# Attention and a routed expert layer on one core: blocks turned two at a time, other places for the expert buffers, longer value rows and a shorter cut of GpSimd's work

## The chip, the cores and the metric

The kernel runs on one core of one Trainium2 chip. The metric is the device time of one execution in microseconds; the kernel before takes 766.43 us (median of three runs, 765.69 to 766.94). Engines are named as the profile names them: PE is TensorE (PEld its weight loads), DVE VectorE, ACT ScalarE, POOL GpSimd, SP the queue that issues most DMAs.

## The reference, cut to what matters

```python
# attention: B=8, H=8, S=576, D=64; a query block of 64 rows sees the key blocks up to its own
scores = scale * np.matmul(q, k.transpose(0, 1, 3, 2))
mask = block_i >= block_j                      # blocks of 64
scores = np.where(mask, scores, -1000000000.0)
attn = np.exp(scores - np.max(scores, axis=-1, keepdims=True))
attn = attn / (np.sum(attn, axis=-1, keepdims=True) + 1e-09)
x = (attn @ v).transpose(0, 2, 1, 3).reshape(B * S, H * D)     # 4608 rows of 512
# one expert of 8 for each row
logits = x @ w_gate + modality_bias[modality_id]
e_idx = np.argmax(logits, axis=1)              # gate_w: softmax of the logits at e_idx
for e in range(E):
    mask = e_idx == e
    h = np.maximum(x[mask] @ w1[e], 0.0)       # 512 -> 1024
    out[mask] = gate_w[mask, None] * (h @ w2[e])   # 1024 -> 512
```

## The kernel before

**Attention** goes through 32 pairs of heads, one pair in a slot; 33 slots are walked, and `ORDER` lists by hand in which order every slot hands work to the engines. Each engine works its own list strictly in that order. The two heads of a pair lie in the two halves of the 128 partitions.

In its slot a pair is taken through these steps (letters as in `ORDER`):

- `S`, `M`, `E` (scores, row maxima, exponentials). The nine query blocks, called subs 0 to 8, have 64 to 576 keys. `PIECES` cuts the scores into ten column stretches, `COL` says in which of the six PSUM banks each stands, and `UNITS` groups them for DVE's maxima and ACT's exponentials. Sub 8 has 576 columns and needs two banks; `CUT` is where it is cut. PE multiplies 64x64 tiles, and the subs in `FLIP` use the other two quarters of its array, so that two subs run side by side. The exponentials go to `pm`, one column stretch for each sub (`OFF`).
- `G`, `g`: nine small gate products from `vt`, copied by ACT into the columns 64 to 71 of each 73-column block of the value tile `v`. The last column of a block is 1, which makes the row sums.
- `T`, `C` (turn and copy). PE transposes `pm` in 128-column blocks, a matmul with the identity as the moving operand, into PSUM; ACT or DVE (`ON_DVE`) copies it to `pt`. `GROUPS` lists the blocks of each of seven groups. An even sub has an odd number of 64-column halves, so its last block has only 64 columns: these five are the half-height blocks, in groups 5 and 6. Group 6 (sub 0 alone) is turned first, into the bank that group 5 uses last.
- `Va`, `Vb`, `Za`, `Zb` belong to the pair of the slot before: PE multiplies `pt` with `v` (50 products), DVE divides by the row sums into `xr`.
- `q...` are the steps of routing (logits, expert, place in the expert's list), mostly small DVE operations, done for a batch while the next batch's slots run. POOL scatters the row numbers by indirect DMA.

**The last seven slots of attention** also prepare the first expert: `EARLY_STEPS` stages its weights through two 128x1024 buffers (`staging`); `prep` lets POOL cast each to float32r (high part) and subtract it from the original (low part), into `extra`. DVE works beside that.

**The expert layer** takes segments of 256 rows: 10 of expert a and c with weights in `extra` (name "a"), 8 and a half of expert b with weights in `w0hb`, `w0lb`, `w1b`. A segment is 8 transposes (`turn_rows`), 96 products of 256 moving columns (`up_products`; stationary: a weight block, moving: `xth` or `xtl`) and 48 products of 512 moving columns (`down`; stationary: a block of `hidden`, moving: the second weights). In `extra` every buffer begins at a multiple of 4,096 bytes from its start. In the program as built, `extra` starts at byte 28,288 of a partition (a multiple of 64), `w0hb` at 156,192 and `w1b` at 188,960 (each 32 more than a multiple of 64).

Of the kernel before, what the change touches and what calls it, by code (L numbers as in the profile page):

```python
# [11 lines left out]
F32 = mybir.dt.float32  # L12
# [38 lines left out]
PIECES = (((7, 0, 512),), ((6, 0, 448), (0, 0, 64)), ((5, 0, 384), (3, 0, 256)), ((8, 0, 256), (4, 0, 320), (8, 256, 576), (2, 0, 192), (1, 0, 128)))  # L51
# [6 lines left out]
GBANK = (0, 1, 2, 3, 4, 5, 5)  # L58
POS = {x: 512 * g + 128 * i for g, group in enumerate(GROUPS) for i, x in enumerate(group)}
# [44 lines left out]
def attention_moe(ctx, tc, qk, vr, vt, gmw, mid, mb, w1, w2, cf, ci, ld, out):  # L104
# [30 lines left out]
    extra = steady.tile([128, 22 * 1024], F32R, name="extra")  # L135
# [14 lines left out]
    pms = [att.tile([128, OFF[-1] + S], F32, name=f"pm{i}") for i in range(2)]  # L150
# [3 lines left out]
    for v in vs:  # L154
        dve.memset(v[:, :, D + NE], 1.0)
    for t in pts:
        dve.memset(t[64:128, 512 * HALF :], 0.0)
# [26 lines left out]
    def place(s, a, b):  # L184
        i, o = COL[s] if a == 0 else (COL[s][0] + 1, -CUT)
        return banks[i][:, o + a : o + b]
# [332 lines left out]
class Experts:  # L519
    def __init__(self, ctx, tc, cst, scratch, btmp, edges, xrows, idlist, idf, w1, w2, out, sel, run, base8, pick, dot, banks, ys, placing, staging, extra, xrb):  # L520
# [223 lines left out]
    def run_all(self, steps):  # L744
# [101 lines left out]
def _prepare(q, k, v, moe_modality_id, moe_w_gate, moe_modality_bias, moe_w1, moe_w2):  # L846
# [28 lines left out]
```

## Time and profile before

| | us |
|---|---|
| median of three runs | 766.43 |
| profiled execution, its own time | 774.59 |
| its span, first to last instruction | 772.9 |
| attention, to the first expert transposes | about 317 |
| one slot, most of them | 9.40 |
| one expert segment, a / b | about 23.3 / 23.6 |

The profiled execution is 8.2 us slower than the median, so durations are summed against 774.59 and the difference is then taken from 766.43. "Busy" of PE counts a matmul's modelled end, so PE looks busy in every stretch where it is fed; the starts of successive instructions tell more. A wait in brackets is the idle time of that engine just before the row, with what ended it.

### The profile page before, as it was taken

The page shows a single profiled execution, that of the slowest core. Times are in us where ns is not written, and L with a number is a line of the kernel's source. Part 1 is how long each engine was busy: PE and PEld are TensorE (multiplying, and loading weights), DVE is VectorE, ACT ScalarE, POOL GpSimd, SP SyncE. Part 2 cuts the span into 40 slices and gives each one's busy share as a digit, 9 for nine tenths or more (in the row PEclk, how much of TensorE's full clock was granted, in tenths as well). Part 3 has the DMA queues.
Part 4 walks back from the last instruction along what each step waited for, and adds up shares of the span by engine and source line. Part 5 has one row for each costly group of instructions (what it writes and reads, how often), then busy time and mean ns, then how long its engine had stood idle before and what let it go on. Part 6 is the DMA issues. An engine that isn't in the chain of part 4 may idle for free. (4 is left out here: it accounts for less than half of the span.)

```text
span 772.9 us, 20835 instructions
## 1 busy us (share of the span) xinstructions
PE 752.9 (97%) x8696; PEld 669.2 (87%) x8696; DVE 371.9 (48%) x1095; ACT 323.0 (42%) x685; POOL 165.4 (21%) x146
## 2 busy tenths in 40 slices
PE   7999999999999999998999999999999999999995
PEld 5888888888888877988999999999999888999894
DVE  4888888888899999643111221111221222221120
ACT  4777776777776766412212222212221222221220
POOL 0000202020202466217223223223112211112101
PEclk9999999999999999998999999999999999999998
DMA  7478565656565969331221221122212212211000
GB/s 206 129 222 229 147 179 149 175 151 177 154 182 132 248 192 268 86 79 36 66 83 69 83 69 70 40 83 70 74 51 83 83 55 69 69 42 46 28 14 19
DMA packets 82625, 85.12 MB, mean 110 GB/s; under 512 B 53002, under 2 KB 64970, under 8 KB 82528
## 3 DMA queue, kind: packets, MB, share of 16 engines
q1 hardware_dynamic: 75040, 64.24, 30.5%
q0 software_dynamic: 7488, 19.52, 7.9%
q8 instruction: 69, 1.13, 0.6%
q14 instruction: 28, 0.23, 0.1%
HBM read 62.09 MB, written 22.25 MB: 109 GB/s over the span
## 5 line engine op out<-in xcount | busy, mean ns | idle before, releaser
L681 DVE SCALAR_TENSOR_TENSOR extra<-bank,extra 128x512 fp32r<-128x512 f32 x72 | 49.8, 691 | 316.7 <-ACT extra L680 316.7
L216 ACT ACTIVATE pm<-bank,nm 128x320 f32<-128x320 f32 (+3 forms) x320 | 137.0, 508 | 70.0 <-DVE nm L208 68.2
L674 PE MATMUL bank<-extra 128*128 128x256 f32 x960 | 121.8, 288 | 2.7 <-issue 2.2
L674 PEld LDWEIGHTS bank<-extra 128*128 128x128 f32 x960 | 119.5, 196 | 5.0 <-issue 3.8
L208 DVE TENSOR_REDUCE nm<-bank 128x1 f32<-128x256 f32 (+7 forms) x288 | 110.8, 444 | 12.0 <-PE bank L200 11.6
L680 ACT ACTIVATE extra<-bank 128x512 fp32r<-128x512 f32 x72 | 43.1, 598 | 165.5 <-PE bank L674 156.6
L226 PE MATMUL bank<-cf,pm 128*128 128x128 f32 (+1 forms) x800 | 95.1, 277 | 2.7 <-ACT pm L216 2.2
L367 POOL DMA_INDIRECT idlist<-idt,pi x40 | 39.4, 986 | 251.6 <-DVE pi L366 162.0
L674 PE MATMUL bank<-extra,w0hb 128*128 128x256 f32 x512 | 92.5, 282 | 0.0
L226 PEld LDWEIGHTS bank<-cf,pm 128*128 128x128 f32 (+1 forms) x800 | 86.6, 136 | 5.8 <-ACT pm L216 3.8
L200 PE MATMUL bank<-raw,q 64*64 64x256 f32 (+7 forms) x1280 | 87.0, 408 | 0.0
L200 PEld LDWEIGHTS bank<-raw,q 64*64 64x64 f32 x1280 | 54.6, 133 | 29.3 <-issue 19.0
L674 PEld LDWEIGHTS bank<-extra,w0hb 128*128 128x128 f32 x512 | 79.2, 188 | 0.7
L231 ACT COPY pt<-bank 128x512 f32<-128x512 f32 (+1 forms) x128 | 64.5, 504 | 27.5 <-PE bank L226 24.8
L250 PE MATMUL o<-v,pt 128*64 128x73 f32 x2048 | 75.1, 228 | 0.0
L674 PE MATMUL bank<-extra,w0lb 128*128 128x256 f32 x256 | 71.9, 281 | 0.0
L231 DVE COPY pt<-bank 128x512 f32<-128x512 f32 (+1 forms) x96 | 64.8, 684 | 14.2 <-PE bank L226 12.8
L250 PEld LDWEIGHTS o<-v,pt 128*64 128x64 f32 x2048 | 70.3, 136 | 0.1
L720 PE MATMUL o<-extra 128*128 128x512 f32 x240 | 57.1, 393 | 0.0
L720 PE MATMUL bank<-extra 128*128 128x512 f32 x240 | 56.0, 389 | 0.0
L720 PEld LDWEIGHTS bank<-extra 128*128 128x128 f32 x240 | 45.0, 188 | 9.4
L720 PE MATMUL o<-w1b,extra 128*128 128x512 f32 x216 | 52.8, 400 | 0.0
(146 smaller groups left out, 819.1 us busy)
## 6 DMA issues: line engine op xcount, KB each, us to landing
raw<-qk SPq DMA_DIRECT2D x31, 576.0 KB
v<-vr SPq DMA_DIRECT2D x32, 320.0 KB
vt<-vt SPq DMA_DIRECT2D x32, 288.0 KB
xrows<-xr SPq DMA_DIRECT2D x16, 576.0 KB
staging<-w SPq DMA_DIRECT2D x24, 256.0 KB
staging<-w SPq DMA_DIRECT2D x12, 512.0 KB
idlist<-btmp SPq DMA_DIRECT2D x8, 304.0 KB
idlist<-idt,pi POOLq DMA_INDIRECT x40
```

Of the source, the lines that this page charges most:

```text
L200: pe.matmul(place(s, a, b)[64 * t : 64 * t + 64], d.q[hs, D * s : D * s + D], d.k[hs, a:b], start=True, stop=True)
L208: dve.tensor_reduce(low, place(s, a, b), AX.X, ALU.max, negate=True)
L216: act.activation(d.pm[:, OFF[s] + a : OFF[s] + b], place(s, a, b), AF.Exp, bias=d.nm[:, s : s + 1], scale=1.0)
L226: pe.transpose(banks[GBANK[g]][0:m, 128 * i : 128 * i + 128], d.pm[:, o : o + m], idf)
L231: dve.tensor_copy(dst, src) if g in ON_DVE else act.copy(dst, src)
L250: pe.matmul(o[64 * h : 64 * h + 64], d.pt[:, a : a + 64], d.v[:, 5 * h + j, :], start=j == 0, stop=j == s // 2)
L367: last = pool.indirect_dma_start(idlist[:], bass.IndirectOffsetOnAxis(ap=g.pi[c], axis=0), g.idt[:, c, :], None, bounds_check=NROW - 1, oo ...
L674: nc.tensor.matmul(hp[:, a, :], w[:, kc, ms], x[:, kc, :], start=i == 0, stop=i == len(mm) - 1)
L680: self.nc.scalar.activation(hh, hp, AF.Relu)
L681: self.nc.vector.scalar_tensor_tensor(hl, hp, 0.0, hh, ALU.max, ALU.subtract)
L720: nc.tensor.matmul(y, s.hs[m][x][:, ts], self.part(w, 1, m // 2)[:, m % 2, :], start=n == 0, stop=n == len(mm) - 1)
```

## The change

Five edits, all in one file:

1. Turning. `pm` gets a new layout: the last 64 columns of sub 6 stand just ahead of sub 0, those of sub 4 just ahead of the last 64 columns of sub 8 (`TAIL`). One 128-column transpose then turns two half-height blocks at once, the second into the upper 64 partitions of the bank. The 25 transposes of a pair become 23. Group 6 has no transposes of its own any more; its copy (`C6`, now 256 columns) reads partitions 64 to 127 of bank 5 and writes partitions 0 to 63 of `pt`, at the end of the turn, and group 5's copy loses a quarter of its columns.
2. Scores. Sub 8 is cut at 512 instead of 256: 512 columns fill bank 4, the last 64 go to bank 5 with subs 3 and 1.
3. Buffers. `extra` is laid out anew, with the first weights of expert a (`w["a", 0]`) last and 32 bytes further; two 32-byte pads stand around `w1b`. As built, `w0hb` is at byte 156,128 (still 32 more than a multiple of 64) and `w1b` at 188,928 (a multiple of 64).
4. Values. The host lays out `v` with its gate columns and ones, so one pair's load is one run of 2,920 bytes a partition instead of ten runs of 256. Three memsets go.
5. `prep`. POOL casts and subtracts in four pieces of 256 columns, a cast and a subtraction in turn.

```diff
+SHIFT = 8
-COL = {7: (0, 0), 6: (1, 0), 0: (1, 448), 5: (2, 0), 4: (3, 0), 2: (3, 320), 3: (4, 0), 8: (4, 256), 1: (5, 320)}
-CUT = 256
+COL = {7: (0, 0), 6: (1, 0), 0: (1, 448), 5: (2, 0), 4: (3, 0), 2: (3, 320), 8: (4, 0), 3: (5, 0), 1: (5, 256)}
+CUT = 512
+LONG = (5, 384)
-OFF = [32 * s * (s + 1) for s in range(NSUB)]
+OFF = {7: 0, 5: 512, 3: 896, 1: 1152, 6: 1280, 0: 1728, 4: 1792, 8: 2176, 2: 2688}
+TAIL = 2112
 GROUPS = (
...
-    ((3, 0), (3, 1), (2, 0), (1, 0)), ((6, 3), (4, 2), (2, 1), (8, 4)), ((0, 0),),
+    ((3, 0), (3, 1), (2, 0), (1, 0)), ((6, 3), (4, 2), (2, 1)), ((0, 0), (8, 4)),
 )
 ORDER = (
...
-    ("T6", 0), ("C6", 0), ("T0", 0), ("C0", 0), ...
+    ("T0", 0), ("C0", 0), ... ("T5", 0), ("C5", 0), ("C6", 0), ...
@@ attention_moe
-    extra = steady.tile([128, 22 * 1024], F32R, name="extra")
+    extra = steady.tile([128, 22 * 1024 + SHIFT], F32R, name="extra")
-    for v in vs:
-        dve.memset(v[:, :, D + NE], 1.0)
@@ load_v
-        nc.sync.dma_start(d.v[:, :, 0:D], vr[p].rearrange("p (a d) -> p a d", d=D))
+        nc.sync.dma_start(d.v.rearrange("p a f -> p (a f)"), vr[p][:, 0 : 10 * VW])
@@ transposes
-        m = height(g)
         for i, (s, j) in enumerate(GROUPS[g]):
             o = OFF[s] + 128 * j
-            pe.transpose(banks[GBANK[g]][0:m, 128 * i : 128 * i + 128], d.pm[:, o : o + m], idf)
+            m = 64 if s == 2 and j == 1 else 128
+            pe.transpose(banks[g][0:m, 128 * i : 128 * i + 128], d.pm[:, o : o + m], idf)
@@ copies
+        if g < HALF:
+            dst, src = pt[:, 512 * g : 512 * g + n], banks[g][:, 0:n]
+        elif g == HALF:
+            dst, src = pt[0:64, LOW : LOW + n], banks[HALF][0:64, 0:n]
+        else:
+            dst, src = pt[0:64, LOW + 384 : LOW + 384 + n], banks[HALF][64:128, 0:n]
@@ Experts
-        self.w["a", 0] = [cut(4096 * x, 4, 4096) for x in range(2)]
-        self.w["a", 1] = [[cut(1024 * (8 + 4 * x + c), 2) for c in range(4)] for x in range(2)]
-        self.xth, self.xtl = cut(1024 * 16, 4), cut(1024 * 17, 4)
-        self.hidden = [[cut(1024 * (18 + i) + 512 * x, 2, 512) for x in range(2)] for i in range(4)]
+        self.w["a", 1] = [[cut(1024 * (4 * x + c), 2) for c in range(4)] for x in range(2)]
+        self.xth, self.xtl = cut(1024 * 8, 4), cut(1024 * 9, 4)
+        self.hidden = [[cut(1024 * (10 + i) + 512 * x, 2, 512) for x in range(2)] for i in range(4)]
+        self.w["a", 0] = [cut(1024 * 14 + SHIFT + 4096 * x, 4, 4096) for x in range(2)]
@@ early, "prep"
-            self.nc.gpsimd.tensor_copy(self.target(k, name, c)[0], st)
-            self.lower(True)
+            flat = [t.rearrange("p a f -> p (a f)") if len(t.shape) > 2 else t for t in (st, *self.target(k, name, c))]
+            for i in range(4):
+                s, h, l = (t[:, 256 * i : 256 * i + 256] for t in flat)
+                self.nc.gpsimd.tensor_copy(h, s)
+                self.nc.gpsimd.tensor_tensor(l, s, h, ALU.subtract)
+            self.staged.pop(0)
@@ run_all
+        wk.tile([128, SHIFT], F32R, name="pad0")
         w2 = [wk.tile([128, 2, DM], F32R, name=f"w1b{i}") for i in range(8)]
+        wk.tile([128, SHIFT], F32R, name="pad1")
```

How the instructions stand now. On PE, the turn of one pair and the first scores of the next slot, before (`bank_90` to `bank_95` are the six banks in order, `pm` the exponentials, `cf` holds the identity; 64x128 is a half-height block; a wait stands in brackets):

```order
L250 MATMUL b_97<-v_104,pt_109 64x73 x17
L226 MATMUL bank_95<-cf,pm_108 64x128 [waits Activation_49]
L226 MATMUL bank_90<-cf,pm_108 128x128 x4
L226 MATMUL bank_91<-cf,pm_108 128x128 x4
L226 MATMUL bank_92<-cf,pm_108 128x128 x4
L226 MATMUL bank_93<-cf,pm_108 128x128 x4
L226 MATMUL bank_94<-cf,pm_108 128x128 x4
L226 MATMUL bank_95<-cf,pm_108 64x128 [waits Activation_49]
L226 MATMUL bank_95<-cf,pm_108 64x128 x3
L200 MATMUL bank_90<-raw_98,q_100 64x512 [waits DMAHW3_49,Activation_49]
```

and the same place in the change (its lines are numbered otherwise: L255 was L250, L225 was L226, L201 was L200):

```order
L255 MATMUL b_97<-v_104,pt_109 64x73 x17
L225 MATMUL bank_90<-cf,pm_108 128x128 x4
L225 MATMUL bank_91<-cf,pm_108 128x128 x4
L225 MATMUL bank_92<-cf,pm_108 128x128 x4
L225 MATMUL bank_93<-cf,pm_108 128x128 [waits Activation_49]
L225 MATMUL bank_93<-cf,pm_108 128x128 x3
L225 MATMUL bank_94<-cf,pm_108 128x128 x3
L225 MATMUL bank_94<-cf,pm_108 128x128 [waits Activation_49]
L225 MATMUL bank_95<-cf,pm_108 128x128 x2
L225 MATMUL bank_95<-cf,pm_108 64x128
L201 MATMUL bank_90<-raw_98,q_100 64x512 [waits DMAHW3_49,Activation_49]
```

Two transposes are gone, and the first wait for ACT's exponentials stands twelve transposes later. On ACT, from the last exponentials of a pair to the first of the next, before (`q` is the scaled query, `nm` the negated maxima):

```order
L216 ACTIVATE pm_107<-bank_95,nm 128x128 [waits Activation_49]
L182 ACTIVATE q_101<-raw_99 128x576 [waits DMAHW6_49,Activation_49]
L231 COPY pt_109<-bank_95 64x128 [waits PE_49]
L231 COPY pt_109<-bank_90 128x512 [waits PE_49,Activation_49]
L231 COPY pt_109<-bank_92 128x512 [waits PE_49,Activation_49]
L231 COPY pt_109<-bank_94 128x512 [waits PE_49,Activation_49]
L216 ACTIVATE pm_108<-bank_90,nm 128x512 [waits DVE_49]
```

and in the change:

```order
L218 ACTIVATE pm_107<-bank_95,nm 128x128 [waits Activation_49]
L183 ACTIVATE q_101<-raw_99 128x576 [waits DMAHW6_49,Activation_49]
L236 COPY pt_109<-bank_90 128x512 [waits PE_49,Activation_49]
L236 COPY pt_109<-bank_92 128x512 [waits PE_49,Activation_49]
L236 COPY pt_109<-bank_94 128x512 [waits PE_49]
L236 COPY pt_109<-bank_95 64x256 [waits DVE_49]
L218 ACTIVATE pm_108<-bank_90,nm 128x512 [waits DVE_49]
```

The copy of group 6 moved from the head of the copies to their end, is twice as wide, and waits for DVE, whose copy of group 5 reads the other half of the same bank.

## Rows read from the trace of the kernel before

**Rows 1.** Windows, a slot: length, busy PE, PEld, DVE, ACT, POOL; clock, DMA share, GB/s.
```profile
17.10:26.50 9.40, 9.40 (x188) 8.19 (x187) 7.83 (x22) 6.85 (x17) 0.00 (x0) 1.00 0.44 130
```

**Rows 2.** Timeline of PE in that slot: start us, us, instruction, idle before.
```profile
17.08 2.69 PE L200 MATMUL bank<-raw,q 64*64 64x512 f32 x40
...
23.63 2.92 PE L226 MATMUL bank<-cf,pm 128*64 128x128 f32 x25
26.48 1.08 PE L200 MATMUL bank<-raw,q 64*64 64x512 f32 x8
```

**Rows 3.** Timeline of PE's weight loads, part of a turn: full blocks, half blocks.
```profile
166.90 1.23 PEld L226 LDWEIGHTS bank<-cf,pm 128*128 128x128 f32 x11
...
168.75 0.33 PEld L226 LDWEIGHTS bank<-cf,pm 128*64 128x64 f32 x3
```

**Rows 4.** Groups by form: ACT's copies of the turn, busy us and mean ns.
```profile
L231 ACT COPY pt<-bank 128x512 f32<-128x512 f32 x96 | 56.3, 586 | 25.5 <-PE bank L226 23.6 <-issue 0.9 <-ACT pt L231 0.6
...
L231 ACT COPY pt<-bank 64x128 f32<-64x128 f32 x32 | 8.2, 257 | 2.0 <-PE bank L226 1.2
```

**Rows 5.** Timeline of PEld and DVE where a slot begins.
```profile
159.87 0.21 PEld L200 LDWEIGHTS bank<-raw,q 64*64 64x64 f32 x8 [0.20 <-issue]
160.05 0.68 DVE L231 COPY pt<-bank 64x512 f32<-64x512 f32 x1 [0.25 <-PE bank L226]
```

**Rows 6.** Timeline of PE and DVE where the slot of the expert choice begins.
```profile
236.10 0.40 PEld L200 LDWEIGHTS bank<-raw,q 64*64 64x64 f32 x8 [0.20 <-issue]
236.58 1.27 DVE L231 COPY pt<-bank 128x512 f32<-128x512 f32 x2
```

**Rows 7.** Waits: who for whom, us in all, times, longest.
```profile
PEld bank L226 <- ACT pm L216: 3.8, 8, 2.3
```

**Rows 8.** Timeline of the first slot, PE and ACT.
```profile
9.63 0.72 PE L238 MATMUL b<-gm,vt 128*64 128x16 f32 x18 [0.58 <-DMA vt<-vt]
...
10.94 1.56 ACT L216 ACTIVATE pm<-bank,nm 128x256 f32<-128x256 f32 x4
12.39 0.69 ACT L182 ACTIVATE q<-raw 128x576 f32<-128x576 f32 x1
12.56 4.58 PE L226 MATMUL bank<-cf,pm 128*64 128x128 f32 x25 [2.21 <-ACT pm L216]
```

**Rows 9.** Windows: the turn of the first slot.
```profile
12.50:17.10 4.60, 4.54 (x29) 4.35 (x29) 1.38 (x2) 2.24 (x6) 0.00 (x0) 0.63 0.74 217
```

**Rows 10.** Timeline around 283 us: POOL, DVE, PE.
```profile
282.79 2.36 POOL L618 TENSOR_TENSOR extra<-staging,extra 128x1024 fp32r<-128x1024 f32 x1
282.99 2.17 DVE L366 TENSOR_TENSOR pi<-pp,cf 128x1 int32<-128x1 f32 x1
286.18 0.44 PE L291 MATMUL b<-l,cf 128*128 128x72 f32 x2 [1.48 <-DVE l L288]
```

**Rows 11.** Timeline around 303 us: DVE, PE.
```profile
302.96 2.27 DVE L333 TENSOR_SCALAR sm<-sm 128x5 f32<-128x5 f32 x1
307.57 0.20 PE L326 MATMUL b<-oh,ones 128*128 128x40 bf16 x1 [1.39 <-DVE row L563]
```

**Rows 12.** Timeline of PE: a segment of expert a, then parts of two of b.
```profile
505.06 5.73 PE L720 MATMUL o<-extra 128*128 128x512 f32 x24
516.06 11.68 PE L674 MATMUL bank<-extra 128*128 128x256 f32 x96
527.57 1.03 PE L656 MATMUL bank<-cf,xr 128*128 128x128 f32 x8
539.36 0.40 PE L674 MATMUL bank<-extra,w0hb 128*128 128x256 f32 x2
550.88 1.04 PE L656 MATMUL bank<-cf,xr 128*128 128x128 f32 x8
551.67 5.87 PE L720 MATMUL o<-w1b,extra 128*128 128x512 f32 x24
562.99 0.40 PE L674 MATMUL bank<-extra,w0hb 128*128 128x256 f32 x2
```

More of the change, by code (lines that the diff above doesn't have):

```diff
@@ L47 @@
 UNITS = ((7,), (6, 0), (5,), (4, 2), (3, 8, 1))
-COL = {7: (0, 0), 6: (1, 0), 0: (1, 448), 5: (2, 0), 4: (3, 0), 2: (3, 320), 3: (4, 0), 8: (4, 256), 1: (5, 320)}
-CUT = 256
+COL = {7: (0, 0), 6: (1, 0), 0: (1, 448), 5: (2, 0), 4: (3, 0), 2: (3, 320), 8: (4, 0), 3: (5, 0), 1: (5, 256)}
+CUT = 512
+LONG = (5, 384)
 FLIP = (6, 0, 5, 4, 2)
-PIECES = (((7, 0, 512),), ((6, 0, 448), (0, 0, 64)), ((5, 0, 384), (3, 0, 256)), ((8, 0, 256), (4, 0, 320), (8, 256, 576), (2, 0, 192), (1, 0, 128)))
-OFF = [32 * s * (s + 1) for s in range(NSUB)]
+PIECES = (((7, 0, 512),), ((6, 0, 448), (0, 0, 64)), ((5, 0, 384), (8, 0, 512)), ((4, 0, 320), (3, 0, 256), (2, 0, 192), (8, 512, 576), (1, 0, 128)))
+OFF = {7: 0, 5: 512, 3: 896, 1: 1152, 6: 1280, 0: 1728, 4: 1792, 8: 2176, 2: 2688}
+TAIL = 2112
 GROUPS = (
     ((7, 0), (7, 1), (7, 2), (7, 3)), ((6, 0), (6, 1), (6, 2), (5, 0)), ((5, 1), (5, 2), (4, 0), (4, 1)), ((8, 0), (8, 1), (8, 2), (8, 3)),
-    ((3, 0), (3, 1), (2, 0), (1, 0)), ((6, 3), (4, 2), (2, 1), (8, 4)), ((0, 0),),
+    ((3, 0), (3, 1), (2, 0), (1, 0)), ((6, 3), (4, 2), (2, 1)), ((0, 0), (8, 4)),
 )
 HALF = 5
-GBANK = (0, 1, 2, 3, 4, 5, 5)
-POS = {x: 512 * g + 128 * i for g, group in enumerate(GROUPS) for i, x in enumerate(group)}
+LOW = 512 * HALF
+POS = {x: 512 * g + 128 * i - 128 * (g > HALF) for g, group in enumerate(GROUPS) for i, x in enumerate(group)}
 ON_DVE = (1, 3, 5)
@@ L149, in attention_moe @@
     vs = [att.tile([128, 10, VW], F32, name=f"v{i}") for i in range(3)]
-    pms = [att.tile([128, OFF[-1] + S], F32, name=f"pm{i}") for i in range(2)]
+    pms = [att.tile([128, D * NSUB * (NSUB + 1) // 2], F32, name=f"pm{i}") for i in range(2)]
     pts = [att.tile([128, 25 * 128], F32, name=f"pt{i}") for i in range(2)]
@@ L153, in attention_moe @@
     dve.memset(zeros, 0.0)
-    for v in vs:
-        dve.memset(v[:, :, D + NE], 1.0)
     for t in pts:
-        dve.memset(t[64:128, 512 * HALF :], 0.0)
+        dve.memset(t[64:128, LOW:], 0.0)
     scatters, placing = [], []
@@ L184, in place @@
     def place(s, a, b):
-        i, o = COL[s] if a == 0 else (COL[s][0] + 1, -CUT)
-        return banks[i][:, o + a : o + b]
+        i, o = COL[s] if a == 0 else LONG
+        return banks[i][:, o : o + b - a]
     def spans(s):
@@ L215, in exps @@
             for a, b in spans(s):
-                act.activation(d.pm[:, OFF[s] + a : OFF[s] + b], place(s, a, b), AF.Exp, bias=d.nm[:, s : s + 1], scale=1.0)
-    def height(g):
-        return 64 if g >= HALF else 128
+                o = OFF[s] if a == 0 else TAIL
+                act.activation(d.pm[:, o : o + b - a], place(s, a, b), AF.Exp, bias=d.nm[:, s : s + 1], scale=1.0)
     def transposes(p, g):
         d = pairs[p]
-        m = height(g)
         for i, (s, j) in enumerate(GROUPS[g]):
             o = OFF[s] + 128 * j
-            pe.transpose(banks[GBANK[g]][0:m, 128 * i : 128 * i + 128], d.pm[:, o : o + m], idf)
+            m = 64 if s == 2 and j == 1 else 128
+            pe.transpose(banks[g][0:m, 128 * i : 128 * i + 128], d.pm[:, o : o + m], idf)
     def copies(p, g):
-        m, n = height(g), 128 * len(GROUPS[g])
-        dst, src = pairs[p].pt[0:m, 512 * g : 512 * g + n], banks[GBANK[g]][0:m, 0:n]
+        pt = pairs[p].pt
+        n = 128 * len(GROUPS[g])
+        if g < HALF:
[4 more added lines that the diff above has]
+            dst, src = pt[0:64, LOW + 384 : LOW + 384 + n], banks[HALF][64:128, 0:n]
         dve.tensor_copy(dst, src) if g in ON_DVE else act.copy(dst, src)
@@ L850, in _prepare @@
     vp = v.reshape(NPAIR, 2, S, D)
-    vr = np.zeros((NPAIR, 128, 2, 5, D), v.dtype)
-    vr[:, :, :, 0:4] = vp[:, :, 0:512].reshape(NPAIR, 2, 4, 128, D).transpose(0, 3, 1, 2, 4)
-    vr[:, 0:64, :, 4] = vp[:, :, 512:576].transpose(0, 2, 1, 3)
+    vr = np.zeros((NPAIR, 128, 2, 5, VW), v.dtype)
+    vr[..., VW - 1] = 1
+    vr[:, :, :, 0:4, 0:D] = vp[:, :, 0:512].reshape(NPAIR, 2, 4, 128, D).transpose(0, 3, 1, 2, 4)
+    vr[:, 0:64, :, 4, 0:D] = vp[:, :, 512:576].transpose(0, 2, 1, 3)
     gmw = np.zeros((2, D, PPB, 2 * NE), moe_w_gate.dtype)
```

2 lines of the change are left out of this document (1 added, 1 removed), and 2 rows, old and new, of the table ORDER.

## The prediction, made before the result was known

> **What bounds the kernel now.** I read the page's slices first, then the windows of one slot, PE's timeline in it, the waits, and last the timelines of the first slot, of the slots in which POOL prepares weights, and of two expert segments. In the slices the reader is to see PE full from one end to the other, and in an ordinary attention slot the window says it outright: PE 9.40 of 9.40 us, DVE 7.83, ACT 6.85 [rows 1]. The slot runs from one pair's first score product at 17.08 to the next one's at 26.48; the turn starts at 23.63 and fills what is left [rows 2]. So PE's own instructions set the time of attention, and DVE has some 1.6 us of slack a slot. The expert layer is PE alone.
>
> **Turning in twos.** It removes four half-height transposes a pair and makes two others full: 25 become 23. What a half-height one is worth is the point: three half loads in a row take 0.33 us, eleven full ones 1.23 [rows 3]. That is 0.11 us each, both ways; the identity that streams through is 128 columns long in either. Two fewer are 0.22 us a slot, over 32 slots 7.0 us, all on the path. The slot should come to 9.18. The Trainium skill ("TensorE: Matmul & The Clock Gate", section LDWEIGHTS) says that a load costs by its stationary columns, so that a half block would cost half: by it 22.5 block loads stay 22.5 and the sum would lose the 7.0. The rows above speak against it here, since the halves are no closer together than the whole ones.
>
> The scores keep their ten pieces and 2,880 columns a head; the two quarters of the array get 1,472 and 1,408 columns as before, so I price the new cut of sub 8 at nothing on PE. On ACT and DVE it trades 256 + 320 columns for 512 + 64, which their slack hides.
>
> **The copy that moved.** Group 6's copy grows from 128 to 256 columns: between 257 and 586 ns [rows 4], by the line between them 0.37 us, 0.11 more. It now stands last in ACT's turn copies and waits for DVE's copy of group 5. Behind it on ACT are the next pair's exponentials, which wait for maxima anyway; on PE the pieces of bank 5 (subs 3, 8's tail, 1) wait for it, and everything behind them. DVE's copy ends 0.86 us after the slot's start (159.87 to 160.73) [rows 5], and loses a quarter of its columns; so group 6 is copied by about 1.2. PE asks for bank 5 at about 1.6: in its quarter 1,024 of 1,472 columns go ahead, of some 2.4 us, and the weights load a little earlier (an estimate from the scores' row). That leaves 0.35 us of slack. It is gone where routing holds DVE up: in the slot of the expert choice, begun at 236.10, DVE's last copy ends at 237.85 [rows 6], so group 6 ends near 2.0 and PE loses 0.4. I charge 0.6 for this slot and three lesser ones; the ends are nothing and the whole 7.0. A copy from one partition half to the other is not in the trace before; see the slower rival.
>
> **The first wait of the turn.** Before, the first transpose used bank 5 and so waited for the pair's last exponential. Now twelve transposes, 1.3 us, go ahead of the first such wait. The view of waits has 3.8 us in eight such waits, the longest 2.3 [rows 7]; that one is the first slot. The other seven make 1.5; part of each is a pause that PE makes between products and transposes anyway, so I take 0.9 (ends 0 and 1.5).
>
> **The first slot** has no products of an earlier pair to fill PE. The gates end at 10.35 (9.63 + 0.72), the turn starts at 12.56 after 2.21 us idle, ACT's last exponential ends at 12.50 (10.94 + 1.56) and its scaling of the next query at 13.08 [rows 8]. In the change twelve transposes run from 10.4 to 11.7, sub 8's wait until its exponential at about 12.0, the last until 12.5, and the turn ends near 13.1. The next scores then wait for ACT's first copy, 13.08 + 0.59 = 13.7 [rows 4], instead of 17.08. Of these 3.3 us, 0.2 are counted above and 0.4 go because banks 2 and 4 are copied only by 14.3 and 14.9. I take 2.7. The old turn also ran in part at the lower of PE's two clock levels: the granted clock was 0.63 over that stretch, after the idle time before it [rows 9]. With that idle time mostly gone I expect 2.4 GHz; at 1.2 GHz over the new turn and the scores behind it the gain would be 1.0, so the ends are 1.0 and 3.1.
>
> The value loads become fewer, longer runs; nobody waits for them in an ordinary slot, and the DMA engines are at 0.44 [rows 1], so: nothing. ACT's gate copy must now wait for its pair's load, with the last exponentials behind it; the load is issued a slot ahead, so that too is nothing, except in the first slot, within the bounds just given. The three memsets stood under DVE's wait for the first query.
>
> **POOL in four pieces.** At 282.99 a DVE operation on one column took 2.17 us, until POOL's subtraction of 2.36 us was over; PE then waited 1.48 us for DVE [rows 10]. At 302.96 the same happened to a five-column one, 2.27 us, and PE waited 1.39 us [rows 11]. A quarter of the subtraction is 0.6 us, and that much DVE's 1.6 us of slack absorbs. I take both waits as gone, 2.9 us; the ends are nothing (if POOL's pieces follow so closely that DVE gets no turn between them) and 2.9. What eight instructions instead of two cost POOL is not shown; between two preparations it mostly waits for DMAs, so I price it at nothing.
>
> **The expert buffers.** The same 48 down products take 11.00 us in a segment of expert a (505.06 to 516.06) and 11.32 in one of b (551.67 to 562.99) [rows 12]. Instructions and shapes are alike; what differs is where the operands lie: in a, `hidden` and the second weights both start at multiples of 64 bytes, in b the weights start 32 further. The change puts `w1b` at a multiple of 64, so I expect b to become like a: 0.32 us in eight and a half segments, 2.7 us. The 96 up products take 11.51 us in a (516.06 to 527.57) and 11.52 in b (539.36 to 550.88) [rows 12], where the weights already stand 32 bytes off; so moving a's to 32 off is worth nothing. No row shows the new addresses themselves. The only address effect in sight is 0.32 of 11.0, 2.9%: for the ups of 18 segments that is 6.0 us either way, and for a's down products, whose distance modulo 64 stays, 3.2 the wrong way.
>
> The Trainium skill ("TensorE: Matmul & The Clock Gate", section Step-by-step: what each phase is for) gives weight loads and moving operand a read port each and says that one doesn't slow the other. By that the pads would do nothing and the 2.7 us go. The row has a difference between a and b that it does not explain, hence my choice, but the rule stands as a rival.
>
> **Sum.** 7.0 + 0.9 + 2.7 + 2.9 - 0.6 + 2.7 = 15.6 us. The profiled execution's 774.59 would become 759.0; the runs' median is 8.2 lower, and I take the same 15.6 from it: 766.43 - 15.6 = 750.8.
>
> **Rivals.**
> - The pads do nothing (the rule on read ports): 15.6 - 2.7 = 12.9 us, 753.5. For it: up products don't care about 32 bytes. Against it: the 0.32 us. Chance 0.20.
> - The turn's saving does not come, because bank 5 comes free 0.2 us too late in every slot or because half blocks were cheap: 750.8 + 7.0 = 757.8. Against it: 0.35 us of slack, and the spacing of the half loads. Chance 0.08.
> - POOL's pieces still shut DVE out: 750.8 + 2.9 = 753.7, and later still where several DVE operations are hit in a row. For it: DVE runs many small operations there. Chance 0.06.
> - The new places quicken the up products too: 6.0 us at 2.9%, 744.8; if they came down to the transposes' 0.11 us from 0.12, 96 products by 18 segments would give 17 us, 733. Nothing in the rows calls for it, but nobody would see it there either. Chance 0.10.
> - Slower: ACT's copy from the upper partitions to the lower ones costs far more than its size. From 0.72 us on (0.37 + 0.35) PE waits for bank 5 in each of 32 slots, and from 1.21 us on (15.6 / 32 more) the kernel is slower than before; at 1.3 us it would be 32 x 0.58 = 18.6 against 15.6, 769.4. Against it: the widest copy of the turn takes 0.59 us. Chance 0.04.
>
> The forecast keeps 0.52, with a range of its own of 747 to 754. The range of 743 to 758 takes in all but the slower rival and the far end of the quicker one. A measurement of this kernel can tell about 0.2%, 1.5 us, from no change; the slower rival is all that lies beyond it upward, 0.04, some mixture of failures could end near 766, 0.03, and 0.93 is left for faster.
>
> **What would show it.** In the profile after: ordinary slots 9.18 us apart; 23 transposes; the first slot's next scores near 13.7; granted clock at full in the first slot; no DVE operation of 2 us near 283 or 303 us, and no PE wait for routing there; b's 48 down products in 11.0 us; ups still 11.5. Slots that stay at 9.40 with PE waiting at bank 5 would prove the second rival, or the last. Slots of 9.18 with a segment of b still 11.32 would prove the first.

## The result, and the profile after

The kernel after takes 753.29 us (median of six runs, 752.61 to 756.76) where the kernel before takes 767.0 (six runs, 765.69 to 769.10): a ratio of 0.983, 95% interval 0.981 to 0.985. The forecast was 750.8, the range 743 to 758. The profiled execution took 752.61, span 751.0. From the starts on PE, stretch by stretch, in us (slots are counted from 0):

| stretch | before | after | less |
|---|---|---|---|
| to the first score product | 6.36 | 5.42 | 0.9 |
| first slot | 10.72 | 7.71 | 3.0 |
| next 25 slots | 239.22 | 234.46 | 4.8 |
| slots 26 to 30 (POOL prepares weights) | 51.41 | 47.52 | 3.9 |
| last slot, to the first ups | 11.14 | 11.18 | 0.0 |
| first ups to last downs | 434.27 | 424.48 | 9.8 |
| rest | 19.8 | 20.2 | -0.4 |

These 22 us are more than the 13.7 of the medians. The profiled execution before was 8.2 above the median shown with it, and 6.3 us of the expert layer's 9.8 are one stall in it, near 355 us, that the profile after does not have (below). The 0.9 at the start is no part of the change either: the kernel after has 6.25 there in its second profile. Without these two about 15 are left. An ordinary slot after, first the window with the columns of [rows 1], then PE's timeline:

```profile
22.50:31.72 9.22, 9.22 (x186) 7.96 (x185) 8.39 (x28) 7.07 (x17) 0.00 (x0) 1.00 0.44 139
```

```profile
31.69 2.70 PE L201 MATMUL bank<-raw,q 64*64 64x512 f32 x40
...
38.25 2.73 PE L225 MATMUL bank<-cf,pm 128*128 128x128 f32 x23
40.91 1.50 PE L201 MATMUL bank<-raw,q 64*64 64x512 f32 x16
```

The slot is 9.22 (31.69 to 40.91), not 9.40, and the turn 2.73 instead of 2.92 [rows 2]. PE still sets it. The first slot, where [rows 8] has the turn from 12.56 to 17.1, and its window:

```profile
9.72 1.53 PE L225 MATMUL bank<-cf,pm 128*128 128x128 f32 x12
11.62 1.42 PE L225 MATMUL bank<-cf,pm 128*128 128x128 f32 x11 [0.38 <-ACT pm L218]
13.14 1.07 PE L201 MATMUL bank<-raw,q 64*64 64x512 f32 x10
```

```profile
9.72:13.14 3.42, 2.95 (x26) 2.45 (x24) 2.11 (x6) 3.17 (x10) 0.00 (x0) 1.00 1.00 376
```

Twelve transposes go ahead of the exponentials that were the first wait, and the granted clock is 1.00 where [rows 9] has 0.63. The moved copy and the waits around it, from the groups by form and the view of waits:

```profile
L236 ACT COPY pt<-bank 64x256 f32<-64x256 f32 x32 | 11.8, 369 | 15.1 <-DVE pt L236 15.0
```

```profile
ACT pt L236 <- DVE pt L236: 15.0, 31, 1.6
PEld bank L201 <- ACT pt L236: 1.0, 3, 0.5
PEld bank L225 <- ACT pm L218: 0.6, 1, 0.6
```

It takes 0.37 us, and ACT waits for DVE 31 times; PE only three times. [Rows 7]'s 3.8 us are now 0.6. The dearest of the three is in slot 22:

```profile
208.63 3.42 PE L201 MATMUL bank<-raw,q 64*64 64x512 f32 x40
208.91 0.65 DVE L350 RECIPROCAL wt<-sm 128x80 f32<-128x80 f32 x1
209.48 1.08 DVE L236 COPY pt<-bank 128x512 f32<-128x512 f32 x2
210.65 0.37 ACT L236 COPY pt<-bank 64x256 f32<-64x256 f32 x1 [1.65 <-DVE pt L236]
```

A routing step stands ahead of DVE's last two copies, so group 6 is copied at 211.0, and the scores take 3.42 instead of 2.70. Near 283 us, where [rows 10] has a DVE operation of 2.17:

```profile
283.29 0.73 POOL L562 TENSOR_TENSOR extra<-staging,extra 128x256 fp32r<-128x256 f32 x1
283.80 0.23 DVE L371 TENSOR_TENSOR pi<-pp,cf 128x1 int32<-128x1 f32 x1
```

And the expert segments that answer to [rows 12], expert a first, then b:

```profile
496.12 11.52 PE L683 MATMUL bank<-extra 128*128 128x256 f32 x96
507.48 1.03 PE L665 MATMUL bank<-cf,xr 128*128 128x128 f32 x8
508.27 5.73 PE L729 MATMUL o<-extra 128*128 128x512 f32 x24
...
519.28 0.40 PE L683 MATMUL bank<-extra,w0hb 128*128 128x256 f32 x2
...
531.34 5.82 PE L729 MATMUL o<-w1b,extra 128*128 128x512 f32 x24
...
542.57 0.40 PE L683 MATMUL bank<-extra,w0hb 128*128 128x256 f32 x2
...
553.84 1.04 PE L665 MATMUL bank<-cf,xr 128*128 128x128 f32 x8
```

From start to start: a's ups 11.36 (were 11.51), a's downs 11.01 (11.00), b's downs 11.23 (11.32), b's ups 11.27 (11.52; over the eight segments 11.26 to 11.40). So b's downs did **not** come down to 11.0, and the ups, predicted to stay at 11.5, did change. That is the open question.

### The profile page after: what moved, and what is told of

Read it like the earlier page. It is cut to its first block, busy times and chain, and to the rows that moved or that the text cites. A ratio compares the mean times of both kernels' runs of the same rounds, so it can differ in the third digit from the quotient of the medians.

```text
span 751.0 us, 20660 instructions
## 1 busy us (share of the span) xinstructions
PE 736.7 (98%) x8632; PEld 653.9 (87%) x8632; DVE 362.9 (48%) x1092; ACT 328.9 (44%) x685; POOL 172.3 (23%) x194
## 5 line engine op out<-in xcount | busy, mean ns | idle before, releaser
L218 ACT ACTIVATE pm<-bank,nm 128x64 f32<-128x64 f32 (+3 forms) x320 | 135.9, 504 | 49.4 <-DVE nm L209 45.4
L209 DVE TENSOR_REDUCE nm<-bank 128x1 f32<-128x512 f32 (+7 forms) x288 | 119.5, 475 | 15.6 <-PE bank L201 15.3
L683 PE MATMUL bank<-extra 128*128 128x256 f32 x960 | 116.1, 281 | 1.2 <-ACT extra L668 0.9
L683 PEld LDWEIGHTS bank<-extra 128*128 128x128 f32 x960 | 115.0, 188 | 2.4 <-issue 1.1
L225 PE MATMUL bank<-cf,pm 128*128 128x128 f32 (+1 forms) x736 | 87.7, 275 | 0.4 <-ACT pm L218 0.4
L201 PE MATMUL bank<-raw,q 64*64 64x64 f32 (+7 forms) x1280 | 87.7, 409 | 0.1
L225 PEld LDWEIGHTS bank<-cf,pm 128*128 128x128 f32 (+1 forms) x736 | 78.9, 139 | 3.2 <-ACT pm L218 0.6
L201 PEld LDWEIGHTS bank<-raw,q 64*64 64x64 f32 x1280 | 53.0, 133 | 31.7 <-issue 24.2
L236 ACT COPY pt<-bank 128x512 f32<-128x512 f32 (+1 forms) x128 | 67.4, 535 | 28.3 <-DVE pt L236 15.0
L255 PE MATMUL o<-v,pt 128*64 128x73 f32 x2048 | 75.3, 228 | 0.2 <-issue 0.2
L255 PEld LDWEIGHTS o<-v,pt 128*64 128x64 f32 x2048 | 70.4, 136 | 0.5 <-issue 0.3
L236 DVE COPY pt<-bank 128x512 f32<-128x512 f32 (+1 forms) x96 | 60.9, 640 | 7.3 <-PE bank L225 2.9
L732 POOL DMA_INDIRECT out<-scratch,ids_b x17 | 17.1, 1003 | 161.7 <-ACT scratch L731 161.7
L729 PEld LDWEIGHTS bank<-extra 128*128 128x128 f32 x240 | 45.0, 188 | 9.4
```

What stands on the lines that cost most here:

```text
L201: pe.matmul(place(s, a, b)[64 * t : 64 * t + 64], d.q[hs, D * s : D * s + D], d.k[hs, a:b], start=True, stop=True)
L209: dve.tensor_reduce(low, place(s, a, b), AX.X, ALU.max, negate=True)
L218: act.activation(d.pm[:, o : o + b - a], place(s, a, b), AF.Exp, bias=d.nm[:, s : s + 1], scale=1.0)
L225: pe.transpose(banks[g][0:m, 128 * i : 128 * i + 128], d.pm[:, o : o + m], idf)
L236: dve.tensor_copy(dst, src) if g in ON_DVE else act.copy(dst, src)
L255: pe.matmul(o[64 * h : 64 * h + 64], d.pt[:, a : a + 64], d.v[:, 5 * h + j, :], start=j == 0, stop=j == s // 2)
```

## The experiments

Each stood beside runs of the kernel before on its own chip; that kernel alone was 767 us beside the result and on chip 9, and 772 on chips 1, 4 and 8, so ratios are compared, and stretches of traces. "Last slot" is the stretch from the start of slot 31 to the first ups, 11.2 us in the profile after.

**Products alone.** Two kernels that only multiply: blocks of ups (`w` stationary, `x` streamed) and of downs (`h`, in the place of `x`, stationary, `d`, in the place of `w`, streamed), with one pair of starting places after another. `x` and `h` are operand 1, moved by `f` words, `w` and `d` operand 2, moved by `g`.

```diff
+for n, (f, g) in enumerate(SHIFTS):
...
+                    pe.matmul(banks[a % 2][:, 0:256], w[u][:, kc, ms], x[v][:, kc, :], start=i == 0, stop=i == len(mm) - 1)
...
+                    pe.matmul(banks[2 + a], h[m // 2][x][:, m % 2, 128 * a : 128 * a + 128], d[u][:, m, :], start=i == 0, stop=i == len(mm) - 1)
```

> Products alone: nothing of attention, routing or experts is computed, only 22 times 48 up-like products (128x128 weights, 256 moving columns) and 48 down-like ones (512 moving columns), one pair of starting places after another. The weights of the ups (the moving operand of the downs) start 0, 4, 8, 16, 24, 32, 48, 64, 96, 128, 192, 216, 224, 232, 256, 384, 512 and 768 words of 4 bytes past a common place; the last four pairs move the other operand by 8, both by 8, the other by 224, and none. Theory (places modulo 64 bytes): distances of 0, 16, 32, 48 ... words are alike, 8 and 24 are alike and differ from them: downs near 227 ns at the first kind and 234 at the second, ups 120 and 118. Rival 1 (places matter, but modulo something longer): 224 words, the distance that expert b's second weights have to the hidden rows in the kernel after, gives 234 ns for downs although it is a multiple of 64 bytes, and 0 gives 227. Rival 2 (places do not matter, the rule that weight loads and moving operand have a port each): all distances within 1 ns, and what differs in the kernels comes from the other engines, which stand still here.

> Products alone again (48 up-like and 24 down-like ones for each set of places; nothing of attention, routing or experts is computed). Four places are moved apart: the high and the low part of the operand that the ups stream (both also the weights of the downs), and the high and the low part of the other. In words of 4 bytes: (0,0,0,0); both parts of the first operand by 2, 4, 6, 8, 10, 12, 16, 24, 32, 40, 48, 56, 60, 72, 136, 264; then (8,0,0,0), (0,8,0,0), (8,16,0,0), (8,40,0,0), (0,0,0,8), (0,0,8,0), (0,0,0,32), (8,8,0,8), (8,8,8,0), (8,8,0,32), (8,8,0,56), (8,8,256,256), (0,0,24,24), (0,0,216,216). Theory (the distance of the two operands modulo 64 words, that is 256 bytes, sets the spacing): 72, 136 and 264 give what 8 gives, 116.7 ns for ups, 216 what 24 gives, and no place gives downs under 226.7. Rival (absolute places or longer distances count too): they differ by over 1 ns from what 8 gives.

PE's timelines of the first (operand 2 moved by 216, then by 224) and of the second (operand 1 by 40, then by 48):

```profile
195.06 5.80 PE L51 MATMUL bank<-buf 128*128 128x256 f32 x48
200.69 11.38 PE L57 MATMUL bank<-buf 128*128 128x512 f32 x48
211.91 5.92 PE L51 MATMUL bank<-buf 128*128 128x256 f32 x48
217.67 11.36 PE L57 MATMUL bank<-buf 128*128 128x512 f32 x48
```

```profile
122.39 5.86 PE L51 MATMUL bank<-buf 128*128 128x256 f32 x48
128.08 5.75 PE L56 MATMUL bank<-buf 128*128 128x512 f32 x24
133.67 5.62 PE L51 MATMUL bank<-buf 128*128 128x256 f32 x48
139.12 5.66 PE L56 MATMUL bank<-buf 128*128 128x512 f32 x24
```

Start to start over 48, the ups take 117.3 and 120.0 ns, then 118.5 and 113.5: no other engine works. By how far operand 1 lies past operand 2, in words of 4 bytes, modulo 64, the spacing from start to start, where it repeats steadily, is:

| | 0 | 8 | 16 | 24 | 32 | 40 | 48 | 56 | 60 |
|---|---|---|---|---|---|---|---|---|---|
| ups, ns | 120.0 | 116.7 | 117.8 | 120.0 | 118.7 or 120.0 | 117.3 or 118.7 | 113.3 or 117.8 | 118.4 | 117.1 or 118.3 |
| downs, ns | 226.7 | 233.2 | 233.3 | 234.3 | 232.2 or 233.5 | 233.3 | 228.9 | 233.3 | 226.7 or 231.8 |

Moves by 72, 136 and 264 give what 8 gives, 224 what 96 and 32 give: the period is 64 words, **256 bytes**, and the first theory (64 bytes) is wrong; rival 1 is right. Both operands moved by 8 give what 0 gives, so it is the distance that counts. Moves by 2 to 12 words, and the high and the low part moved apart, gave 117.6 to 120.0 ns for ups and 230 to 234 for downs: nothing quicker than the table has. Some places have two values: the spacing is a short cycle, and which one PE falls into differs from block to block. The kernels fit into the table: ups of a at 0 before and 56 after, ups of b at 24 and 40 (in the kernel after 11.27 us in one segment, 117.4 ns, and 11.39 in another), downs of a at 0 in both, downs of b at 24 and at 32. The Trainium skill ("TensorE: Matmul & The Clock Gate", section Step-by-step: what each phase is for) lets weight loads and the streamed operand read through ports of their own without loss; by that the table would be flat. It is not, by 6% for ups; why the distance counts no run here shows.

**The old places.**

```diff
-self.w["a", 0] = [cut(1024 * 14 + SHIFT + 4096 * x, 4, 4096) for x in range(2)]
+self.w["a", 0] = [cut(4096 * x, 4, 4096) for x in range(2)]
...
-wk.tile([128, SHIFT], F32R, name="pad0")
...
-wk.tile([128, SHIFT], F32R, name="pad1")
```

> The kernel after with the expert buffers placed as in the kernel before (no shift, no pads, first weights of a first). Theory (places set the spacing of PE's products): a segment of a goes back to 11.0 + 11.5 us, its ups to 120 ns from 118.3; a segment of b to 120 ns for ups, downs 236 instead of 234; ten segments of a lose 0.15 each, eight of b 0.25 each: 3.5 us slower than the kernel after, about 756.8. The prediction as it stood: only b's downs change, 2.7 us, about 756.0. Rival (the places do nothing; the ups became quicker through POOL's pieces or something else): ups stay at 118, and the time at 753.3.

```profile
509.28 11.68 PE L682 MATMUL bank<-extra 128*128 128x256 f32 x96
520.80 1.04 PE L664 MATMUL bank<-cf,xr 128*128 128x128 f32 x8
```

a's ups are back at 11.52, b's ups too, and b's downs at 11.32. The rival falls. The time, 766.91 (0.993 of before), is 10 us above the 756.8 expected: its profile holds two stalls of the kinds described below, 6.3 us in the first full segment and 3.7 in the last slot. The second run of the kernel after, below, has both too, and takes 763.76 on another chip with the same time before: 3.1 less, where the theory has 3.5.

**Other places.** From the table: downs of both experts at 0, ups of both at 48.

```diff
-SHIFT = 8
+SHIFT = 16
-wk.tile([128, SHIFT], F32R, name="pad0")
+wk.tile([128, 48], F32R, name="pad0")
-wk.tile([128, SHIFT], F32R, name="pad1")
+wk.tile([128, 40], F32R, name="pad1")
```

> The kernel after with other places alone: first weights of expert a 16 words past the multiple of 1024 instead of 8, pads of 48 and 40 words instead of 8 and 8 about b's buffers. So both experts' second weights start a multiple of 64 words (256 bytes) from the hidden rows, and both experts' first weights lie such that the turned rows start 48 words past them, modulo 64. Theory (the distance modulo 64 words sets the spacing, as in the products alone): b's 48 downs 10.78 us instead of 11.01; ups between 113.3 and 117.8 ns instead of 118.3 and 117.4 to 118.7, by where in its cycle a block begins: 96 ups in 10.8 to 11.2 us; in all 2.5 to 10 us faster than the kernel after, ratio to before 0.976 to 0.985 where the kernel after gave 0.9885. Rival (only what each engine does beside PE counts): b's downs stay at 11.0.

```profile
564.03 1.04 PE L665 MATMUL bank<-cf,xr 128*128 128x128 f32 x8
564.82 5.73 PE L729 MATMUL o<-w1b,extra 128*128 128x512 f32 x24
...
575.83 0.40 PE L683 MATMUL bank<-extra,w0hb 128*128 128x256 f32 x2
```

b's downs take 11.01, as a's: what the change was predicted to reach. The ups fell into the slower cycle, 117.8 ns everywhere, so 96 take 11.3 us and not the expected 10.8 to 11.2. Ratio 0.985 (0.982 to 0.987).

**POOL's preparation whole.**

```diff
...
-for i in range(4):
-    s, h, l = (t[:, 256 * i : 256 * i + 256] for t in flat)
-    self.nc.gpsimd.tensor_copy(h, s)
-    self.nc.gpsimd.tensor_tensor(l, s, h, ALU.subtract)
...
+self.nc.gpsimd.tensor_copy(self.target(k, name, c)[0], st)
+self.lower(True)
```

> The kernel after with POOL's preparations whole again: one cast and one subtraction of 1024 columns instead of four pieces of 256. Theory: DVE operations of 2 us come back in the slots 28 to 30 of attention, and PE waits for routing there as before: 1.9 us in slot 28, 1.5 in slot 30, so 3 us slower than the kernel after, about 756.3; nothing else moves. Rival (the waits of those slots went because the turn's new order shifted DVE's operations away from POOL's subtractions): slots 28 to 30 keep 9.40, 9.53 and 9.99, time 753.3.

```profile
287.30 2.35 POOL L623 TENSOR_TENSOR extra<-staging,extra 128x1024 fp32r<-128x1024 f32 x1
287.75 1.96 DVE L320 TENSOR_TENSOR eq<-eq,cf 128x40 f32<-128x40 f32 x1
```

DVE's forty columns take 1.96 us and end 0.06 after POOL's subtraction, and PE's scores in slot 30 then wait 1.0 us for DVE's copies behind them. Slots 28 to 30 take 9.57, 10.52, 10.92; in the first profile of the kernel after 9.40, 9.53, 9.99, in the second 9.53, 9.35, 9.27: 2.1 and 2.9 us less. Only slot 30 shows the mechanism. The 1.9 us expected in slot 28 did not come, and 0.95 of slot 29 is a pause of PE for which the profile shows no wait. The Trainium skill ("SBUF — State Buffer", section SBUF: two separate sides) has a DVE operation on two SBUF inputs and a POOL operation that reads SBUF share a pair of ports, which the one that starts first holds for its whole instruction; these rows agree.

Its ratio is 0.985, its time 760.92: 2.8 us **less** than the second run of the kernel after, on a chip with the same time before. Its last slot is 11.1 where that one's is 15.7; the section on the row gathers comes back to this.

**The turn undone.** The kernel before with the other three parts; against the kernel after, `GROUPS`, `COL`, `CUT`, `OFF` and what uses them are as before:

```diff
-    ... ("T0", 0), ("C0", 0), ("T1", 0), ("C1", 0), ...
+    ... ("T6", 0), ("C6", 0), ("T0", 0), ("C0", 0), ("T1", 0), ("C1", 0), ...
...
-    ... ("T5", 0), ("C5", 0), ("C6", 0), ("qp", 1), ("q6", 1),
+    ... ("T5", 0), ("C5", 0), ("qp", 1), ("q6", 1),
```

> The kernel before with the other three parts (buffers, value loads, POOL's pieces) and without the new turn, scores and copies: the new turn undone. Theory (the turn is worth 0.18 us in each of 31 slots, 0.14 more in seven, 3.0 in the first, less 0.9 for the late copy of group 6): about 8.7 us slower than the kernel after, 762.0; ordinary slots of 9.40, first slot 10.7. Rival (the first slot's 3.0 us come from the value loads, which take PE's operands sooner): first slot 7.7 here too, 759.0.

```profile
11.89 5.54 PE L225 MATMUL bank<-cf,pm 128*64 128x128 f32 x25 [1.92 <-ACT pm L215]
17.36 2.88 PE L199 MATMUL bank<-raw,q 64*64 64x512 f32 x40
```

Ordinary slots are 9.40 again and the first slot 11.9: the rival, that the value loads shorten it, falls. It is 1.2 longer than the 10.7 expected, mostly since the granted clock was 0.50, the lower level, over the whole of this turn (5.54 us; [rows 8] has 4.58 at 0.63). Slots 28 and 30 are 9.93 and 9.49 where they were 11.33 and 11.48, so POOL's pieces help without the new turn too, by 3.4 us. 770.65 us, ratio 0.998 (0.996 to 0.999), where 762.0 was expected: besides the first slot, its profile holds stalls as below, 5.0 us in the first full segment and 3.9 in the last slot.

**The old value loads.**

```diff
-nc.sync.dma_start(d.v.rearrange("p a f -> p (a f)"), vr[p][:, 0 : 10 * VW])
+nc.sync.dma_start(d.v[:, :, 0:D], vr[p].rearrange("p (a d) -> p a d", d=D))
```

> The kernel after with the value loads as before: twenty short runs a partition instead of one, and the memsets of the ones. Theory (nobody waits for them): no slot changes, the first slot stays at 7.7, and the time is that of the kernel after within 0.2%. Rival (the many short packets hold up other transfers of the first slot and of the slots in which weights are staged): first slot 8 to 10 us, slots 28 to 30 longer, 1 to 3 us in all.

(The short runs are ten a partition, not twenty; the host's layout and the memsets are the old ones too.) Ratio 0.991 (0.987 to 0.994), the kernel after on the same chip 0.989 (0.986 to 0.991): not told apart. Ordinary slots are alike and the first is 7.98; slot 30 was 15.69 in its profile: PE waits 3.5 us for `vt`, and the 62 value products behind that take 4.04 us instead of 2.17, at a granted clock of 0.50. Kernels with the new loads show that wait too, up to 1.8 us. What the loads are worth stays open.

**The routing step put later**, to free DVE in slot 22.

```diff
-    ... ("C2", 0), ("q5", 1), ("T3", 0), ...
+    ... ("C2", 0), ("T3", 0), ...
...
-    ... ("C6", 0), ("qp", 1), ("q6", 1),
+    ... ("C6", 0), ("q5", 1), ("qp", 1), ("q6", 1),
```

> The kernel after, with the routing step that stands between the second and the third turn copy put behind the last one: nothing else. Theory (in slot 22 DVE's reciprocal of 0.65 us stands ahead of its copies of groups 3 and 5, so group 6 is copied 0.7 us too late for PE; in slot 24 the same with 0.45 us): slot 22 comes down from 10.00 to 9.3, slot 24 from 10.40 to about 9.9, 1.1 us in all, near the bound of what can be measured. Rival (PE waits there for routing anyway): slot 22 stays at 10.0, or another routing step is late and a later slot grows by as much.

```profile
52.82 0.44 PE L296 MATMUL b<-l,cf 128*128 128x72 f32 x2 [1.07 <-DVE l L293]
```

Slot 22 came down from 10.00 to 9.54 (9.3 expected), but the same place in other slots sums the logits for PE: slots 4, 8, 12 and so on grew from 9.40 to 10.73. The rival holds; 770.34 us, ratio 0.998.

**The kernel after again, and the stall.**

> The kernel after once more, beside the kernel before on the same chip. The sum of the terms as the trace after shows them (turn 5.6 + 1.0, first slot 3.0, POOL 3.4, expert buffers 3.5, late copy of group 6 -0.9) is 15.6 us, a ratio of 0.980; the runs so far gave 0.983. If stretches in which PE gets its instructions slowly (6.3 us in the profiled run of before near 354 us, none in that of after) belong to one of the two kernels, the ratio here falls to 0.975 or below; if they come and go in both, it stays between 0.978 and 0.986, and the profile here may have one.

763.76 us beside 772.01, ratio 0.989 (0.986 to 0.991): the gain is smaller there, and outside both of the ranges expected. The trace shows where: the 96 ups of the first full segment take 17.6 us (11.4 in the first profile), and the last slot is 4.6 longer (15.7). PE's timeline, then POOL's:

```profile
338.86 7.34 PE L683 MATMUL bank<-extra 128*128 128x256 f32 x60
346.40 0.28 PE L683 MATMUL bank<-extra 128*128 128x256 f32 x1 [0.19 <-issue]
347.12 0.50 PE L683 MATMUL bank<-extra 128*128 128x256 f32 x2 [0.44 <-issue]
...
356.50 1.44 PE L665 MATMUL bank<-cf,xr 128*128 128x128 f32 x8
```

```profile
341.22 0.97 POOL L372 DMA_INDIRECT idlist<-idt,pi  x1 [0.30 <-DVE mx_c L389]
342.49 0.97 POOL L372 DMA_INDIRECT idlist<-idt,pi  x1 [0.30 <-DVE start L740]
...
348.87 0.97 POOL L372 DMA_INDIRECT idlist<-idt,pi  x1 [0.30 <-issue]
```

PE waits for nothing that the profile shows ("issue") and starts one or two products each 0.7 us, while POOL issues seven indirect transfers 1.27 us apart. In the profile before it is the same place:

```profile
354.86 0.49 PE L674 MATMUL bank<-extra 128*128 128x256 f32 x2 [0.43 <-issue]
```

Two tests: the seven scatters left out of the kernel after, and, on top of the other places, the scatters spaced by a small clearing on POOL.

```diff
-    while self.placing:
-        g, c = self.placing.pop(0)
-        g(c)
+    self.placing.clear()
```

```diff
     while self.placing:
         g, c = self.placing.pop(0)
         g(c)
+        self.nc.gpsimd.memset(self.spare, 0.0)
```

> The kernel after without the last seven index scatters (the tokens of the last batch element are then missing in the lists of rows): nothing else is left out. Theory (that train of indirect transfers is what starves PE of instructions): the 96 ups of the first full segment take 11.2 us, not 17.4. Rival (another cause at that place of PE's program): 16 to 18 us.

> As the run with the new places, and behind each of the last seven index scatters of attention POOL clears 128 by 512 words that nobody reads, so that the scatters no longer follow one another at once. Theory (while POOL issues one indirect transfer right after the other, PE gets its instructions late: four each 0.7 us): the 96 ups of the first full segment, 17.4 us in the last run of the kernel after, take 11.2 or less; 5 to 6 us faster than without the spaces. Rival 1 (PE's instructions are late there for a reason of PE's own): the segment keeps its 6 us. Rival 2 (the later end of the scatters delays the lists, and with them the rows of the next segments): PE waits for rows instead, no gain.

PE's rows without the scatters, then with them spaced, and POOL's there:

```profile
340.21 11.61 PE L681 MATMUL bank<-extra 128*128 128x256 f32 x96
351.65 1.03 PE L663 MATMUL bank<-cf,xr 128*128 128x128 f32 x8
```

```profile
339.02 11.55 PE L684 MATMUL bank<-extra 128*128 128x256 f32 x96
350.41 1.04 PE L666 MATMUL bank<-cf,xr 128*128 128x128 f32 x8
```

```profile
341.38 0.97 POOL L372 DMA_INDIRECT idlist<-idt,pi  x1 [0.30 <-DVE mx_c L389]
342.35 0.54 POOL L591 MEMSET spare<- 128x512 f32 x1
343.06 0.97 POOL L372 DMA_INDIRECT idlist<-idt,pi  x1 [0.17 <-issue]
```

Both take 11.4 us; the unspaced kernel with the other places took 16.4 on the same chip. In eight of the nine profiles with unspaced scatters these ups take 16.4 to 17.9 us (the ninth is the first profile of the kernel after), in the three with them spaced or left out 11.4. So PE's stall hangs on the train of transfers, and 0.4 us more between them was enough: 754.04 against 760.18 us, with no overlap of the single runs. The ratio, 0.977 (0.976 to 0.978), is the lowest of all, but on a chip where the kernel before takes 772; the time is no better than the 753.29 of the result.

**The row gathers spaced as well.**

```diff
 self.gather(s, row)
+self.nc.gpsimd.memset(self.scratch[:, 512:1024], 0.0)
```

> As the run with the new places and the spaced scatters, and POOL also clears 128 by 512 words of scratch behind each of the four row gathers of the last attention slots. Theory (three gathers one after the other make PE's instructions late in the last slot, 4.5 us between the second to last slot's end and the first ups): from the end of slot 30 to the first up products 11.2 us instead of 15.8, span about 749, ratio to before 0.971 where the chip's before is near 772. Rival (the rows come later than the turn that reads them, since the third and fourth gather start 0.4 and 0.8 us later): PE waits at the turn for rows, ratio 0.977 as without them.

The last slot is 11.1 us (15.8 without), as the theory has it. But slot 30 itself was 12.8: PE waited 1.76 us for `vt`, and the 62 value products behind that took 3.52 us instead of 2.18, at a granted clock of 0.54. 753.26 us where before is 766.87, ratio 0.982 (0.979 to 0.984); neither 0.971 nor the rival's 0.977. On a chip whose kernel before takes 767 us there is thus nothing gained over the kernel after.

The run also stood on another chip than the one without the spaces, and beside the result, where before takes 767 too, the unspaced kernel after had a last slot of 11.2. So this run alone does not show that the spacing did it. The other profiles speak for it. POOL's gathers, first in the second run of the kernel after, then with POOL's preparation whole:

```profile
300.07 1.02 POOL L644 DMA_INDIRECT xr<-xrows,row  x1 [0.30 <-DVE nm L209]
```

```profile
298.69 1.02 POOL L640 DMA_INDIRECT xr<-xrows,row  x1 [3.17 <-DVE row L568]
```

With the whole preparation, as in the kernel before, the second and third gather wait for their rows and stand 1.7 us or more behind the one ahead; the last slot is 11.1 in both, in the first of them on the chip where the old places have 14.9 and the old turn 15.0. With POOL's pieces they no longer wait for their rows and follow at 1.3 to 1.4 us, and the last slot takes 12.1 to 16.1 in eight of nine profiles. The ninth is again the first profile of the kernel after.

An inference that fits the times: on chips 1, 4 and 8 all seven unspaced profiles have the scatters' stall. The kernel before takes 5 us more there than beside the result, about one stall; the kernel after takes 10.5 more, and its second profile has two, 6.2 and 4.6. By this, POOL's pieces cost more there, in the last slot, than they bring.

## Why the prediction was right, and where not

- **Turning in twos**: right, a little dear. 0.18 us a slot instead of 0.22; the 30 ordinary slots give 5.4, not 7.0 (32 slots; the first is counted below, the last one gained nothing). A half block did cost nearly what a whole one costs.
- **First wait of the turn**: slots that were 9.67 are 9.35, 0.14 beyond the 0.18; seven of them 1.0 (predicted 0.9).
- **First slot**: 3.0 (2.7), at full clock. The next scores start at 13.14 and not 13.7, but the slot itself began 0.9 sooner; from its own start they are 0.4 later than worked out.
- **The moved copy**: 0.37 us as interpolated. The cost of 0.6 was 0.7 in slot 22 and about 0.1 in slot 26; the place named, the slot of the expert choice, lost little.
- **POOL in pieces**: 11.33 and 11.48 became 9.40 and 9.99; less the turn's 0.18 each, 3.1 (2.9). Pricing the eight instructions at nothing was wrong: they take POOL 4.6 us a buffer instead of 3.5, and the gathers behind them then follow one another at once. In the first profile of the kernel after nothing came of that, in the second the last slot was 4.6 us longer.
- **The expert buffers**: the size was near (3.5 for 2.7: the expert layer's 9.8 less the stall's 6.3), the step was wrong, and the size is luck. It read "in b the weights start 32 further" and set `w1b` "at a multiple of 64, so I expect b to become like a". Two places that agreed modulo 64 bytes were taken for a rule; the period is 256 bytes, `w1b` then stood 128 bytes off, and b's downs gained 0.09 of the 0.32 us. That is 0.8 us. The other 2.7 us came from ups at 117.4 to 118.7 ns for 120, through places of which the prediction expected nothing.
- **Sum**: the terms as measured, 5.4 + 1.0 + 3.0 + 3.1 - 0.8 + 3.5 = 15.2, stand by the predicted 15.6, as the others together make up for most of the 1.6 that the turn was too dear; the medians differ by 13.7. The profiled execution before, less its stall, is 768.3, 1.3 above the six runs' median, of which the later start is 0.9; the one after is the shortest of its six runs, 0.7 below their median. So some runs hold something that this profile does not show; stalls as above would do it, but those runs have no trace.
- **Rivals**: "the pads do nothing" named 753.5 and came closest to the measured 753.3, yet its mechanism is refuted: the time alone would have crowned the wrong theory. "The new places quicken the up products too" happened, at nearly half of its 6.0 us.

## What to carry to other kernels

Where two executions of the same instructions differ by 3%, vary the places one by one in a small kernel of products before making a rule of the one pair that is at hand. Where an engine idles and the profile shows nothing that it waits for, look at what another one issues at that time; and read a gain from the stretches of the trace as well as from the total, since a stall in one of the two profiles can be nearly half of the gain. And a chip on which a train of transfers stalls PE can turn the price of one part of a change round.

## What the runs showed of the hardware

- With no other engine at work, the spacing of products with a weight load each depends on the distance of the two operands modulo 256 bytes: 113.3 to 120.0 ns for 256 columns, 226.7 to 234.3 for 512. Products and weight loads fall into a cycle, and the same places can have two.
- A train of POOL's indirect transfers 1.27 us apart goes with pauses of PE for which the profile shows no wait, 5.0 to 6.4 us in all, in eight of nine profiles; with 1.68 us between them, or without them, there were none in three. That PE lacks instructions then is an inference. The Trainium skill ("Runtime: NRT & Kernel Launch", section The ~15µs preamble/postamble breakdown) has instructions fetched through a port of their own; whether that fetch is late in these pauses no run here shows. The kernel after did not have the stall in its first profile, though its scatters stood as close: what decides that is open.
